# Attention and a mixture of experts on one core: 512-wide first-layer products, routing steps among the copies, another token layout, a shorter warm-up

## Chip, cores and metric

The kernel runs on one core of one Trainium2 chip. The metric is the device time of one execution in microseconds (us), as the median of several runs. Engines are named as in the profile: PE (TensorE; PEld is its weight load), DVE (VectorE), ACT (ScalarE), POOL (GpSimd), SP (SyncE).

## What is computed

Causal attention in blocks of 64 (8 batches, 8 heads, 576 rows, 64 columns a head) gives 4608 rows of 512. Each row goes to the one expert of eight with the largest logit, through two layers of weights, and is scaled with that expert's probability.

```python
scores = scale * np.matmul(q, k.transpose(0, 1, 3, 2))
mask = block_i >= block_j
scores = np.where(mask, scores, -1000000000.0)
scores = scores - np.max(scores, axis=-1, keepdims=True)
attn = np.exp(scores)
attn = attn / (np.sum(attn, axis=-1, keepdims=True) + 1e-09)
return np.matmul(attn, v).astype(np.float32)
...
x = np.ascontiguousarray(attn_out.transpose(0, 2, 1, 3)).reshape(B * S, H * D)
...
logits = x @ w_gate + modality_bias[modality_id]
e_idx = np.argmax(logits, axis=1)
logits_s = logits - logits.max(-1, keepdims=True)
probs = np.exp(logits_s)
probs /= probs.sum(-1, keepdims=True) + 1e-09
gate_w = probs[np.arange(N), e_idx]
for e in range(E):
    mask = e_idx == e
...
    h = np.maximum(x[mask] @ w1[e], 0.0)
    out[mask] = gate_w[mask, None] * (h @ w2[e])
```

## The kernel before

**Slots.** The 64 heads are worked in 32 pairs, one pair in a slot (0 to 31), with a last slot 32. `run_slot` goes through the table `ORDER`, a hand-written order of names; each name has a stage, and a name of stage 1 works on the pair of the slot before. Every engine runs its own instructions in the order in which they are written. S0 to S3 (`scores`, L202, PE) fill banks 0 to 5; M0 to M4 (`maxima`, L209, DVE) take row maxima; E0 to E4 (`exps`, L222, ACT) take exponentials with row sums. V (`values`, L248, PE) multiplies the pair before with its values into banks o0 and b0. T0 to T5 (`transposes`, L229, PE) turn the exponentials, C0 to C5 (`copies`, L234; C0, C1, C5 on DVE, the others on ACT) bring them to SBUF. O (`turn_out`, L256 and L257, ACT), D (`inverse`, L274 and L275, DVE), B (`back`, L268, PE: turns the rows back and multiplies with the gate's weights) and Z0, Z1 (`rows`, L287 and L288, DVE) end the pair before. Z stands at the end of the table, so DVE does it at the start of the next slot, ahead of that slot's M0. Q (`scale`, L184) scales the next pair's queries on POOL; pair 0's are scaled on DVE in one operation (L181).

**Routing.** Four pairs make a batch of 576 rows. After the fourth, `routing` gives 19 small steps: logits (L314), their total by PE (L317, into b0), four bias additions (L321 to L324), the maximum, the expert's index, a weight from the exponentials (L336 on ACT, L357 to L373), stores, counts by PE (L353, L354), running sums (L363 to L387). Steps are taken from the list in order, at the names q1 to q6; PE's products wait for the name qp, their readers for qv. Up to three steps are taken at one name when the list is long, when it holds selection steps (`choose`, 22 of them after the third batch), or from slot 29 on. After the last step five scatters are due for each batch: DVE adds (`pi`, L394), and POOL issues an indirect DMA (L395) that writes row numbers into the experts' lists. One scatter is issued at V and one at T3 of each slot while any is due.

**Experts.** From slot 20 on weights are fetched and split into high and low parts (L584, L585 on POOL). The last slot mixes the end of the last pair with the first expert part. A part is 256 rows of one expert; 18 full parts and one of 128 rows follow each other. First layer (`up_products`, L706): for m2 = 0 to 3 one bank holds two halves a; each half sums over kc = 0 to 3 the products w high x x high, w high x x low, w low x x high, 256 columns wide. `up_relu` (L712 ACT, L713 DVE) makes the high and low part of the hidden rows. Then the next part's rows are turned (`turn_rows`, L688 to L692), and the second layer (`down`, L752) takes 2 x 24 products 512 wide. Three banks rotate for the first layer (`s_bank`), two for turned rows (`t_bank`).

**Start.** Twelve warm-up products (L532) run on PE ahead of the first scores.

Of the kernel before, what the change touches and what calls it, by code (L numbers as in the profile page):

```python
# [25 lines left out]
PPB = H // 2  # L26
# [43 lines left out]
ORDER = (  # L70
# [3 lines left out]
)  # L74
# [7 lines left out]
LAST = (  # L82
    ("+turn0", 0), ("V", 1), ("O", 1), ("D", 1), ("+up0", 0), ("+relu", 0), ("+fetch", 0), ("B", 1), ("Z0", 1), ("Z1", 1), ("+steps1", 0), ("+up1", 0), ("+relu", 0),
    ("+place", 0), ("+steps13", 0), ("+up2", 0), ("+relu", 0), ("+place", 0), ("+steps5", 0), ("+up3", 0), ("+place", 0), ("+relu", 0), ("+turn1", 0), ("+fetch", 0), ("+fetch", 0),
)
# [22 lines left out]
def attention_moe(ctx, tc, qk, vr, bkw, mid, mb, w1, w2, cf, ci, ld, out):  # L108
# [160 lines left out]

    def inverse(p):  # L270
        d = pairs[p]
        den = sml.tile([128, NSUB], F32, name="den")
        d.inv = sml.tile([128, NSUB], F32, name="inv")
        dve.scalar_tensor_tensor(den, d.sums, GUARD, d.long, ALU.add, ALU.add)  # L274
        dve.reciprocal(d.inv, den)  # L275

# [22 lines left out]
    def routing(b):  # L299
        xr, gl = xrs[b]  # L300
        g = Pair()
        tot = b0[:, TABLE : TABLE + NSUB * NE].rearrange("p (s e) -> p s e", s=NSUB)
        ps = b0[:, TABLE : TABLE + 80]

        def t(shape, dt=F32, **k):
            return sml.tile(shape, dt, bufs=2, **k)
# [4 lines left out]

        def logits():
            g.l0 = t([128, NSUB, NE], name="l0")
            dve.tensor_reduce(g.l0, gl, AX.X, ALU.add)  # L314

        def total():
            pe.matmul(tot, ii, g.l0, start=True, stop=True)  # L317

        def biased():
            by = bias[:, 5 * b : 5 * b + 5, :]  # L320
# [17 lines left out]
        def hits():  # L338
            dve.tensor_tensor(eq, lg, bc(g.mx), ALU.is_equal)

        def hit_index():
            dve.tensor_tensor(eq, eq, iom40, ALU.mult)

# [31 lines left out]
        def stores():  # L375
            queue = nc.sync
            queue.dma_start(xrows[S * b : S * b + 512, 512:XW].rearrange("(c p) w -> p c w", p=128), g.wt[:, 0:4])
            queue.dma_start(xrows[S * b + 512 : S * b + S, 512:XW], g.wt[64:128, 4])
            g.idt = t([128, 5, IW], I32, name="idt")
            queue.dma_start(g.idt, ci[b].rearrange("p (c w) -> p c w", c=5))  # L380

# [64 lines left out]
    def emit(name, p):  # L446
        one = {
            "L": lambda: load(p), "Q": lambda: scale(p), "V": lambda: values(p), "O": lambda: turn_out(p), "D": lambda: inverse(p), "B": lambda: back(p),
            "Z0": lambda: rows(p, 0), "Z1": lambda: rows(p, 1),
        }  # L450
# [40 lines left out]
    def run_slot(slot):  # L491
# [3 lines left out]
        for name, stage in LAST if slot == NPAIR else ORDER:  # L495
            p = slot - stage
            if placing and slot < NPAIR and name in ("V", "T3"):
                g, c = placing.pop(0)
                g(c)
            for what in EARLY_STEPS.get((slot, name), ()):  # L500
                if ex is None:
                    ex = Experts(ctx, tc, cst, scratch, btmp, con["edges"], xrows, idlist, idf, w1, w2, out, sel, run, base8, pick, dot, banks, (o0, banks[5]), placing, staging, extra, xrb, lambda kind: any(getattr(f, "kind", "") == kind for f in steps))
                ex.early(what)
# [8 lines left out]
            if name[0] == "q":  # L512
                kind = "" if name[1].isdigit() else name
                kinds = (kind,) if kind else ("", "c")
                quick = bool(steps) and getattr(steps[0], "kind", "") == "c"
                for _ in range(1 if kind else 3 if quick else 3 if slot >= HURRIED else 1 + (len(steps) > 20)):
                    if slot > 1 and steps and getattr(steps[0], "kind", "") in kinds:
                        steps.pop(0)()
                continue
# [3 lines left out]
            if name == "Z1" and p % PPB == PPB - 1:  # L523
                steps = steps + routing(p // PPB)
                if p // PPB == EARLY - 1:
                    choose(Later(dve, steps))

    engines = {ET.PE, ET.Activation, ET.DVE, ET.Pool}
# [16 lines left out]
class Experts:  # L545
    def __init__(self, ctx, tc, cst, scratch, btmp, edges, xrows, idlist, idf, w1, w2, out, sel, run, base8, pick, dot, banks, ys, placing, staging, extra, xrb, steps_left):
# [13 lines left out]
        self.w["a", 1] = [[cut(1024 * (4 * x + c), 2) for c in range(4)] for x in range(2)]  # L560
        self.xth, self.xtl = cut(1024 * 8, 4), cut(1024 * 9, 4)
        self.hidden = [[cut(1024 * (10 + i) + 512 * x, 2, 512) for x in range(2)] for i in range(4)]
# [3 lines left out]
    def s_bank(self):  # L566
        self.sbank += 1
        return self.banks[(self.sbank - 1) % 3]

    def t_bank(self):  # L570
        self.tbank += 1
        return self.banks[3 + (self.tbank - 1) % 2]

# [124 lines left out]
    def up_products(self, s, m2):  # L698
        nc = self.nc
        wh, wl = self.w[s.name, 0]  # L700
        hp = self.s_bank().rearrange("p (a t) -> p a t", a=2)
        for a in range(2):
            ms = slice(256 * m2 + 128 * a, 256 * m2 + 128 * a + 128)
            mm = [(w, kc, x) for kc in range(4) for w, x in ((wh, self.xth), (wh, self.xtl), (wl, self.xth))]
            for i, (w, kc, x) in enumerate(mm):
                nc.tensor.matmul(hp[:, a, :], w[:, kc, ms], x[:, kc, :], start=i == 0, stop=i == len(mm) - 1)  # L706
        s.hp.append(hp)

    def up_relu(self, s):
        hh, hl = self.next_hidden()  # L710
        hp = s.hp.pop(0)
# [141 lines left out]


def _constants():
    p, j = np.indices((128, 128))
    late = np.arange(128) < 64
    ranks = np.broadcast_to(np.arange(NE) - NE, (128, 5, NE))
    seen = ranks.copy()
    seen[late, 4] = 100  # L860
    inv = np.zeros((128, 5))
    inv[late, 4] = BIG
    first = np.ones((128, NE, 5))
# [12 lines left out]
    cf = np.concatenate([con[n].reshape(128, -1) for n, _ in PARTS], axis=1).astype(np.float32)  # L876
    at = np.array([0, 128, 256, 384, 448])
    ci = (np.arange(B)[:, None] * S + at)[:, None] + np.arange(128)[None, :, None]
    ci = np.repeat(ci[..., None], IW, axis=3)
# [3 lines left out]
def _prepare(q, k, v, moe_modality_id, moe_w_gate, moe_modality_bias, moe_w1, moe_w2):  # L883
# [11 lines left out]
    ids = moe_modality_id.reshape(B, S)  # L895
    mid = np.zeros((128, B, 5), ids.dtype)
    mid[:, :, 0:4] = ids[:, 0:512].reshape(B, 4, 128).transpose(2, 0, 1)
    mid[:, :, 4] = np.tile(ids[:, 512:576].transpose(1, 0), (2, 1))
    mb = np.broadcast_to(moe_modality_bias.reshape(1, 2 * NE), (128, 2 * NE))
# [13 lines left out]
```

## Time and profile before

| | us |
|---|---|
| median of 3 runs | 742.62 (742.12 to 743.21) |
| profiled execution | 741.8, span 740.1 |
| PE / PEld busy | 723.7 / 630.2 |
| DVE / ACT / POOL busy | 345.7 / 332.4 / 243.5 |

The span begins with the first record of the profile and ends with the last; 1.7 us of the profiled execution lie outside it. The granted clock of PE is 0.996 of full speed on average over the span. Bars in the profile's timeline are merged where one line's instructions follow each other (x96 is 96 of them); the idle time before an instruction stands in brackets with what ended it.

### The profile page before, as it was taken

To read this page: it belongs to the slowest core of one execution; us is meant where nothing else is said; L and a number is where in the kernel's file an instruction comes from. 1 tells how busy PE (TensorE), PEld (TensorE's weight loads), DVE (VectorE), ACT (ScalarE), POOL (GpSimd) and SP (SyncE) were. 2 spreads that over 40 slices of the span, in tenths; PEclk is the share of its full clock that TensorE was granted. 3 is DMA by queue.
4 is the path that set the end of the run, shared out by engine and by line. 5 is a ranking of instruction groups with operands and counts; after the bars stand their busy time and mean duration, and the time that the engine had idled before them with its cause. 6 is when DMAs were issued, how large, how long until landed. Compare 5 with 4: busy or idle time off the path is not lost. (4 is left out here: it accounts for less than half of the span.)

```text
span 740.1 us, 19430 instructions
## 1 busy us (share of the span) xinstructions
PE 723.7 (98%) x7800; PEld 630.2 (85%) x7800; DVE 345.7 (47%) x1038; ACT 332.4 (45%) x974; POOL 243.5 (33%) x326
## 2 busy tenths in 40 slices
PE   8999999999999998999999999999999999999995
PEld 4888888777888887998899988999889988899794
DVE  5888888898899987513122011220222112221220
ACT  5888877777878877221222212321222212222220
POOL 2223342434398964245223222232111221112101
PEclk9999999999999999999999999999999999999998
DMA  5477455545776673313222022222122121201000
GB/s 187 129 208 220 119 170 136 175 106 158 183 226 190 229 211 72 86 59 79 82 72 85 31 86 72 72 72 72 57 72 72 59 86 58 72 29 48 29 15 20
DMA packets 41916, 77.80 MB, mean 105 GB/s; under 512 B 12170, under 2 KB 24266, under 8 KB 41824
## 3 DMA queue, kind: packets, MB, share of 16 engines
q1 hardware_dynamic: 34336, 57.02, 26.7%
q0 software_dynamic: 7488, 19.52, 8.4%
q8 instruction: 62, 1.02, 0.6%
q14 instruction: 30, 0.25, 0.1%
HBM read 54.86 MB, written 22.25 MB: 104 GB/s over the span
## 5 line engine op out<-in xcount | busy, mean ns | idle before, releaser
L713 DVE SCALAR_TENSOR_TENSOR extra<-bank,extra 128x512 fp32r<-128x512 f32 x72 | 49.8, 692 | 317.3 <-ACT extra L712 315.9
L222 ACT ACTIVATE pm<-bank,nm 128x512 f32<-128x512 f32 (+3 forms) x320 | 155.7, 502 | 64.6 <-DVE nm L209 59.0
L209 DVE TENSOR_REDUCE nm<-bank 128x1 f32<-128x512 f32 (+3 forms) x320 | 120.5, 448 | 4.0 <-PE bank L202 4.0
L706 PE MATMUL bank<-extra 128*128 128x256 f32 x960 | 116.0, 281 | 0.0
L706 PEld LDWEIGHTS bank<-extra 128*128 128x128 f32 x960 | 115.1, 188 | 1.0 <-issue 0.2
L712 ACT ACTIVATE extra<-bank 128x512 fp32r<-128x512 f32 x72 | 43.1, 598 | 151.4 <-PE bank L706 148.2
L229 PE MATMUL bank<-cf,pm 128*128 128x128 f32 (+1 forms) x736 | 91.2, 277 | 2.3 <-ACT pm L222 2.2
L184 POOL TENSOR_SCALAR q<-raw 128x144 f32<-128x144 f32 x124 | 68.0, 576 | 70.6 <-DMA raw<-qk 57.5
L706 PE MATMUL bank<-extra,w0hb 128*128 128x256 f32 x512 | 91.1, 280 | 0.0
L202 PE MATMUL bank<-raw,q 64*64 64x512 f32 (+7 forms) x1280 | 90.1, 407 | 0.8 <-POOL wt L373 0.6
L229 PEld LDWEIGHTS bank<-cf,pm 128*128 128x128 f32 (+1 forms) x736 | 78.1, 139 | 12.3 <-ACT pm L222 6.4
L202 PEld LDWEIGHTS bank<-raw,q 64*64 64x64 f32 x1280 | 56.9, 134 | 29.1 <-issue 20.7
L706 PEld LDWEIGHTS bank<-extra,w0hb 128*128 128x128 f32 x512 | 79.0, 188 | 0.7
L248 PE MATMUL b<-pt,v 64*64 64x64 f32 (+3 forms) x896 | 75.6, 266 | 1.0 <-DVE lg L324 0.9
L248 PE MATMUL o<-pt,v 64*64 64x64 f32 (+3 forms) x896 | 71.4, 262 | 1.2 <-DVE gl L288 1.2
L706 PE MATMUL bank<-extra,w0lb 128*128 128x256 f32 x256 | 71.8, 280 | 0.0
L755 POOL DMA_INDIRECT out<-scratch,ids_b x17 | 16.9, 995 | 161.8 <-ACT scratch L754 161.8
L234 DVE COPY pt<-bank 128x512 f32<-128x512 f32 (+1 forms) x96 | 58.9, 640 | 15.5 <-PE bank L229 9.7
L222 ACT ACTIVATION_READ_ACCUMULATOR pm<-bank,nm 128x1 f32 x320 | 65.3, 204 | 0.0
L395 POOL DMA_INDIRECT idlist<-idt,pi x40 | 40.5, 1012 | 65.8 <-DVE pi L394 47.5
L752 PE MATMUL o<-extra 128*128 128x512 f32 x240 | 57.3, 394 | 0.0
L248 PEld LDWEIGHTS b<-pt,v 128*64 128x64 f32 (+1 forms) x896 | 53.9, 136 | 3.6 <-DVE lg L324 1.1
(148 smaller groups left out, 997.0 us busy)
## 6 DMA issues: line engine op xcount, KB each, us to landing
raw<-qk SPq DMA_DIRECT2D x31, 576.0 KB
v<-vr SPq DMA_DIRECT2D x32, 384.0 KB
staging<-w SPq DMA_DIRECT2D x24, 256.0 KB
staging<-w SPq DMA_DIRECT2D x12, 512.0 KB
xrows<-xr SPq DMA_DIRECT2D x16, 256.0 KB
xrows<-xr SPq DMA_DIRECT2D x32, 128.0 KB
idlist<-btmp SPq DMA_DIRECT2D x8, 304.0 KB
xrows<-xr SPq DMA_DIRECT2D x16, 64.0 KB
```

The source lines that it names most:

```text
L184: pool.tensor_scalar(d.q[:, i : i + 144], d.raw[:, i : i + 144], SCALE, None, ALU.mult)
L202: pe.matmul(place(s, a, b)[64 * t : 64 * t + 64], d.q[hs, D * s : D * s + D], d.k[hs, a:b], start=True, stop=True)
L209: dve.tensor_reduce(d.nm[:, i : i + 1], place(s, a, b), AX.X, ALU.max, negate=True)
L222: act.activation(d.pm[:, o : o + b - a], place(s, a, b), AF.Exp, bias=d.nm[:, s : s + 1], scale=1.0, accum_out=total)
L229: pe.transpose(banks[g][0:m, 128 * i : 128 * i + 128], d.pm[:, o : o + m], idf)
L234: dve.tensor_copy(dst, src) if g in ON_DVE else act.copy(dst, src)
L248: pe.matmul(o.rearrange("p (n c) -> p n c", c=64), d.v[rows, h, block, :], x, start=start, stop=stop)
L395: last = pool.indirect_dma_start(idlist[:], bass.IndirectOffsetOnAxis(ap=g.pi[c], axis=0), g.idt[:, c, :], None, bounds_check=NROW - 1, oo ...
L706: nc.tensor.matmul(hp[:, a, :], w[:, kc, ms], x[:, kc, :], start=i == 0, stop=i == len(mm) - 1)
L712: self.nc.scalar.activation(hh, hp, AF.Relu)
L713: self.nc.vector.scalar_tensor_tensor(hl, hp, 0.0, hh, ALU.max, ALU.subtract)
L752: nc.tensor.matmul(y, s.hs[m][x][:, ts], self.part(w, 1, m // 2)[:, m % 2, :], start=n == 0, stop=n == len(mm) - 1)
```

## The change

Five things.

1. **First layer.** x high and x low lie side by side (`xt`), so one product of width 512 with the high weights serves both; the low weights' product with x high stays 256 wide and adds to the bank's low half. One half a fills one bank: 64 instead of 96 products per part. `up_relu` first adds the two halves of a bank on DVE (`hs`), twice, then takes ACT's relu and DVE's difference, twice each, 256 wide. `s_bank` rotates over four banks, `t_bank` over bank 4 and b0.
2. **Layout of the routing.** Each partition holds other tokens (`_tokens`), so that the total is two products of 64 x 40 into bank 5 and the bias is one addition. Hit and index are one step: 18 steps. The index load moves to the first step, four stores instead of two.
3. **Order of the steps.** q1 to q6 stand among the copies, after C1 and around C5, qv after C5; D is split. One step is taken at each name. The chain to the scatters comes first, 13 steps; weights and stores come behind it (and behind `choose`, for the third batch). Scatters are issued at T3 and B instead of V and T3. The last slot takes 1, 7, 5, 5 steps instead of 1, 13, 5.
4. **Warm-up** of 8 products instead of 12.
5. **First queries** scaled in two operations, columns 384 to 575 first.

```diff
-HURRIED = 29
+PLACED = 13
-NWARM = 12
+NWARM = 8
-TABLE = 400
+TABLE = 384
 ORDER = (
-    ("S0", 0), ("S1", 0), ("Q", -1), ("M0", 0), ("qv", 1), ("E0", 0), ...
-    ("L", -2), ("V", 1), ("q1", 1), ("E4", 0), ("O", 1), ("q2", 1), ("q3", 1), ("q4", 1),
...
+    ("T0", 0), ("C0", 0), ("T1", 0), ("C1", 0), ("q1", 1), ("D0", 1), ("q2", 1), ("D1", 1), ("T2", 0), ("C2", 0), ("q3", 1), ("q4", 1), ("T3", 0), ("C3", 0), ("T4", 0), ("C4", 0), ("T5", 0), ("qp", 1), ("C5", 0),
+    ("qv", 1), ("B", 1), ("q5", 1), ("q6", 1), ("Z0", 1), ("Z1", 1),
...
-            dve.tensor_scalar(d.q, d.raw[:, 0:S], SCALE, None, ALU.mult)
+            for i, j in ((384, S), (0, 384)):
+                dve.tensor_scalar(d.q[:, i:j], d.raw[:, i:j], SCALE, None, ALU.mult)
...
-            pe.matmul(tot, ii, g.l0, start=True, stop=True)
+            for t in range(2):
+                pe.matmul(tot[64 * t : 64 * t + 64], ii[:, 64 * t : 64 * t + 64], g.l0[:, 4 * t : 4 * t + 5], start=True, stop=True)
...
-            dve.tensor_tensor(lg[0:64, 0:4], tot[0:64, 0:4], by[0:64, 0:4], ALU.add)
-            dve.tensor_tensor(lg[64:128, 0:2], tot[64:128, 5:7], by[64:128, 0:2], ALU.add)
-            dve.tensor_tensor(lg[64:128, 2:4], tot[64:128, 4:8:3], by[64:128, 2:4], ALU.add)
-            dve.tensor_tensor(lg[:, 4], tot[:, 8], by[:, 4], ALU.add)
+            dve.tensor_tensor(lg, tot, bias[:, 5 * b : 5 * b + 5, :], ALU.add)
...
-            if placing and slot < NPAIR and name in ("V", "T3"):
+            if placing and slot < NPAIR and name in ("B", "T3"):
...
+        self.xt = extra[:, 1024 * 8 : 1024 * 10].rearrange("p (a x t) -> p a x t", a=4, x=2)
+        self.xth, self.xtl = self.xt[:, :, 0], self.xt[:, :, 1]
...
-        return self.banks[(self.sbank - 1) % 3]
+        return self.banks[(self.sbank - 1) % 4]
...
-            mm = [(w, kc, x) for kc in range(4) for w, x in ((wh, self.xth), (wh, self.xtl), (wl, self.xth))]
-            for i, (w, kc, x) in enumerate(mm):
-                nc.tensor.matmul(hp[:, a, :], w[:, kc, ms], x[:, kc, :], start=i == 0, stop=i == len(mm) - 1)
+            low = hp[a][:, 0:SLOT]
+            for kc in range(4):
+                if kc == 3:
+                    nc.tensor.matmul(low, wl[:, kc, ms], self.xth[:, kc], start=False, stop=False)
+                nc.tensor.matmul(hp[a], wh[:, kc, ms], self.xt[:, kc].rearrange("p x t -> p (x t)"), start=kc == 0, stop=kc == 3)
+                if kc < 3:
+                    nc.tensor.matmul(low, wl[:, kc, ms], self.xth[:, kc], start=False, stop=False)
...
-        self.nc.scalar.activation(hh, hp, AF.Relu)
-        self.nc.vector.scalar_tensor_tensor(hl, hp, 0.0, hh, ALU.max, ALU.subtract)
+        sums = [self.cst.tile([128, SLOT], F32, name="hs", bufs=3) for _ in range(2)]
+        for hs, hp in zip(sums, s.hp.pop(0)):
+            self.nc.vector.tensor_reduce(hs, hp.rearrange("p (x t) -> p t x", x=2), AX.X, ALU.add)
+        for a, hs in enumerate(sums):
+            self.nc.scalar.activation(hh[:, a], hs, AF.Relu)
+            self.nc.vector.scalar_tensor_tensor(hl[:, a], hs, 0.0, hh[:, a], ALU.max, ALU.subtract)
```

DVE before, from the copies of the slot that issues the first batch's first scatter to the rows of the pair (pp is the last routing step, pi a scatter's index, xr and gl the rows of Z):

```order
L390 TENSOR_REDUCE pp<-eq 128x5
L234 COPY pt_110<-bank_92 128x512
L234 COPY pt_110<-bank_93 128x512
L274 SCALAR_TENSOR_TENSOR den<-sums,long_67 128x9
L275 RECIPROCAL inv<-den 128x9
L394 TENSOR_TENSOR pi_1307<-pp,cf 128x1
L234 COPY pt_110<-bank_97 128x384
L287 TENSOR_TENSOR xr_82<-o_98,inv 128x5x64
```

DVE after, at the same place, which is one slot earlier:

```order
L236 COPY pt_111<-bank_93 128x512
L391 TENSOR_REDUCE pp<-eq 128x5
L276 SCALAR_TENSOR_TENSOR den<-sums,long_66 128x9
L279 RECIPROCAL inv<-den 128x9
L357 TENSOR_REDUCE sm<-ex 128x5
L360 TENSOR_SCALAR sm<-sm 128x5
L395 TENSOR_TENSOR pi_1168<-pp,cf 128x1
L236 COPY pt_111<-bank_97 128x384
L395 TENSOR_TENSOR pi_1169<-pp,cf 128x1
L372 RECIPROCAL sm<-sm 128x5
L291 TENSOR_TENSOR xr_82<-o_98,inv 128x5x64
```

Two weight steps now stand ahead of the first scatter's index, and a second scatter's index follows the last copy.

POOL before, the five scatters of the second batch among the scalings of the queries (each row of q is one pair's):

```order
L395 DMA idlist<-idt,pi_2550 38912x16
L184 TENSOR_SCALAR q_102<-raw_100 128x144 x4
L395 DMA idlist<-idt,pi_2551 38912x16
L395 DMA idlist<-idt,pi_2552 38912x16
L184 TENSOR_SCALAR q_103<-raw_101 128x144 x4
L395 DMA idlist<-idt,pi_2553 38912x16
L395 DMA idlist<-idt,pi_2554 38912x16
```

POOL after, the same five:

```order
L396 DMA idlist<-idt,pi_2409 38912x16
L396 DMA idlist<-idt,pi_2410 38912x16
L186 TENSOR_SCALAR q_103<-raw_101 128x144 x4
L396 DMA idlist<-idt,pi_2411 38912x16
L396 DMA idlist<-idt,pi_2412 38912x16
L186 TENSOR_SCALAR q_102<-raw_100 128x144 x4
L396 DMA idlist<-idt,pi_2413 38912x16
```

In both programs two scatters stand together on POOL; before they are those of V and T3 of one slot, after they are those of T3 and B.

PE after, the first half a and the beginning of the second of one m2 (before it is one row, `L706 MATMUL bank_94<-extra 128x256 x24`, for both halves):

```order
L710 MATMUL bank_94<-extra 128x512
L712 MATMUL bank_94<-extra 128x256
L710 MATMUL bank_94<-extra 128x512
L712 MATMUL bank_94<-extra 128x256
L710 MATMUL bank_94<-extra 128x512
L712 MATMUL bank_94<-extra 128x256
L709 MATMUL bank_94<-extra 128x256
L710 MATMUL bank_94<-extra 128x512
L710 MATMUL bank_95<-extra 128x512
```

The 24 products of 256 columns are 8 of 512 and 8 of 256, and the two halves lie in two banks.

## Rows read from the trace of the kernel before

**Rows 1.** Windows: length, then PE, PEld, DVE, ACT, POOL busy (instructions), PEclk, DMA.
```profile
14.42:282.99 268.57, 266.42 (x4679) 220.51 (x4679) 236.40 (x791) 213.65 (x759) 132.23 (x221) 1.00 0.60 172
...
323.32:683.95 360.63, 360.63 (x2382) 330.54 (x2380) 73.85 (x135) 87.90 (x140) 89.27 (x77) 1.00 0.22 66
```

**Rows 2.** Timeline of the start; columns: start us, length us, engine, line, operation, idle before.
```profile
0.86 0.40 SPq L170 DMA_DIRECT2D raw<-qk  x1
...
1.33 0.41 SPq L171 DMA_DIRECT2D raw<-qk  x1
...
1.46 5.28 PE L532 MATMUL b<-scratch,ones 128*128 128x512 bf16 x12 [1.46 <-DVE long L160]
...
3.99 0.46 DVE L181 TENSOR_SCALAR q<-raw 128x576 f32<-128x576 f32 x1 [2.55 <-DMA raw<-qk]
...
6.67 2.93 PE L202 MATMUL bank<-raw,q 64*64 64x512 f32 x40
```

**Rows 3.** Timeline at two slot starts: 110.90, an ordinary one, and 119.45 with a scatter.
```profile
110.90 0.60 PE L202 MATMUL bank<-raw,q 64*64 64x512 f32 x2
...
111.28 0.49 DVE L287 TENSOR_TENSOR xr<-o,inv 128x320 f32<-128x320 f32 x1 [0.33 <-PE o L268]
...
118.91 1.05 POOL L395 DMA_INDIRECT idlist<-idt,pi  x1 [8.04 <-DVE pi L394]
...
119.45 0.59 PE L202 MATMUL bank<-raw,q 64*64 64x512 f32 x2
...
120.46 0.49 DVE L287 TENSOR_TENSOR xr<-o,inv 128x320 f32<-128x320 f32 x1 [0.84 <-PE o L268]
...
128.69 0.59 PE L202 MATMUL bank<-raw,q 64*64 64x512 f32 x2
```

**Rows 4.** Waits of the program: us in total, times, longest.
```profile
DVE xr L287 <- PE o L268: 5.5, 12, 1.0
...
DVE xr L287 <- PE bank L202: 3.9, 4, 1.2
```

**Rows 5.** Windows of single slots, from one slot's first score product to the next slot's.
```profile
57.35:66.29 8.94, 8.94 (x172) 7.22 (x162) 7.52 (x28) 6.75 (x26) 2.18 (x4) 1.00 1.00 327
156.19:166.03 9.84, 9.40 (x172) 7.48 (x167) 9.52 (x45) 7.34 (x27) 4.25 (x6) 1.00 0.57 128
...
272.56:282.99 10.43, 9.88 (x173) 8.23 (x165) 8.19 (x33) 7.58 (x27) 4.81 (x8) 1.00 0.79 216
```

**Rows 6.** Timeline of one expert part, from 485.43 to the next part's first product.
```profile
485.43 11.52 PE L706 MATMUL bank<-extra 128*128 128x256 f32 x96
...
496.79 1.03 PE L688 MATMUL bank<-cf,xr 128*128 128x128 f32 x8
...
497.58 5.73 PE L752 MATMUL o<-extra 128*128 128x512 f32 x24
...
503.15 0.61 PE L752 MATMUL bank<-extra 128*128 128x512 f32 x2
...
508.59 0.40 PE L706 MATMUL bank<-extra,w0hb 128*128 128x256 f32 x2
```

**Rows 7.** Groups by line and form: operations of like shape as the new evacuation.
```profile
L713 DVE SCALAR_TENSOR_TENSOR extra<-bank,extra 128x512 fp32r<-128x512 f32 x72 | 49.8, 692 | 317.3 <-ACT extra L712 315.9 <-issue 1.3
...
L209 DVE TENSOR_REDUCE nm<-bank 128x1 f32<-128x512 f32 x64 | 43.6, 681 | 4.0 <-PE bank L202 4.0
...
L287 DVE TENSOR_TENSOR xr<-b,inv 128x256 f32<-128x256 f32 x32 | 13.3, 415 | 0.0
```

**Rows 8.** Groups by line and form: one of the four bias additions.
```profile
L324 DVE TENSOR_TENSOR lg<-b,bias 128x8 f32<-128x8 f32 x8 | 1.3, 167 | 0.1
```

**Rows 9.** Timeline of the last slot, two scatters one after the other.
```profile
291.58 1.00 POOL L395 DMA_INDIRECT idlist<-idt,pi  x1 [0.30 <-DVE pt L234]
...
292.88 0.98 POOL L395 DMA_INDIRECT idlist<-idt,pi  x1 [0.30 <-issue]
...
294.70 0.49 DVE L287 TENSOR_TENSOR xr<-o,inv 128x320 f32<-128x320 f32 x1 [2.21 <-PE bank L688]
```

More of the change, by code (lines that the diff above doesn't have):

```diff
@@ L268, in back, with inverse @@
                         pe.matmul(bank[t : t + 64, VW * i : VW * i + VW], ot[hs, 64 * c : 64 * c + 64], bk[hs, q, :], start=True, stop=True)
-    def inverse(p):
+    def inverse(p, part):
         d = pairs[p]
[L272 to L275, printed above, removed]
+        if part == 0:
+            d.den = sml.tile([128, NSUB], F32, name="den")
+            dve.scalar_tensor_tensor(d.den, d.sums, GUARD, d.long, ALU.add, ALU.add)
+        else:
+            d.inv = sml.tile([128, NSUB], F32, name="inv")
+            dve.reciprocal(d.inv, d.den)
     def rows(p, k):
@@ L301, in routing @@
         g = Pair()
-        tot = b0[:, TABLE : TABLE + NSUB * NE].rearrange("p (s e) -> p s e", s=NSUB)
-        ps = b0[:, TABLE : TABLE + 80]
+        ps = banks[5][:, TABLE : TABLE + 80]
+        tot = ps[:, 0:40].rearrange("p (c e) -> p c e", c=5)
         def t(shape, dt=F32, **k):
@@ L376, in stores @@
             queue = nc.sync
[L377 to L380, printed above, removed]
+            place = xrows[S * b : S * b + S, 512:XW].rearrange("(s p) w -> p s w", p=64)
+            queue.dma_start(place[:, 0:7:2], g.wt[0:64, 0:4])
+            queue.dma_start(place[:, 5], g.wt[0:64, 4])
+            queue.dma_start(place[:, 1:4:2], g.wt[64:128, 1:3])
+            queue.dma_start(place[:, 7:9], g.wt[64:128, 3:5])
         def place_run():
@@ L400, in place_sum @@
             placing.extend((scatter, c) for c in range(5))
-        return [logits, total, biased, top, shifted, hits, expo, hit_index, first, onehot, weight, weight_guard, weight_out, stores, counts, running, place_run, place_pick, place_sum]
+        return [logits, total, biased, top, shifted, hits, first, onehot, counts, running, place_run, place_pick, place_sum, expo, weight, weight_guard, weight_out, stores]
     sel = {}
@@ L447, in emit @@
         one = {
-            "L": lambda: load(p), "Q": lambda: scale(p), "V": lambda: values(p), "O": lambda: turn_out(p), "D": lambda: inverse(p), "B": lambda: back(p),
+            "L": lambda: load(p), "Q": lambda: scale(p), "V": lambda: values(p), "O": lambda: turn_out(p), "D0": lambda: inverse(p, 0), "D1": lambda: inverse(p, 1), "B": lambda: back(p),
             "Z0": lambda: rows(p, 0), "Z1": lambda: rows(p, 1),
@@ L501, in run_slot @@
                 if ex is None:
-                    ex = Experts(ctx, tc, cst, scratch, btmp, con["edges"], xrows, idlist, idf, w1, w2, out, sel, run, base8, pick, dot, banks, (o0, banks[5]), placing, staging, extra, xrb, lambda kind: any(getattr(f, "kind", "") == kind for f in steps))
+                    ex = Experts(ctx, tc, cst, scratch, btmp, con["edges"], xrows, idlist, idf, w1, w2, out, sel, run, base8, pick, dot, banks + [b0], (o0, banks[5]), placing, staging, extra, xrb, lambda kind: any(getattr(f, "kind", "") == kind for f in steps))
                 ex.early(what)
@@ L514, in run_slot @@
                 kinds = (kind,) if kind else ("", "c")
[L515 to L518, printed above, removed]
+                if slot > 1 and steps and getattr(steps[0], "kind", "") in kinds:
+                    steps.pop(0)()
                 continue
@@ L523, in run_slot @@
             if name == "Z1" and p % PPB == PPB - 1:
-                steps = steps + routing(p // PPB)
+                more = routing(p // PPB)
+                steps += more[0:PLACED]
                 if p // PPB == EARLY - 1:
                     choose(Later(dve, steps))
+                steps += more[PLACED:]
     engines = {ET.PE, ET.Activation, ET.DVE, ET.Pool}
@@ L567, in s_bank @@
         self.sbank += 1
-        return self.banks[(self.sbank - 1) % 3]
+        return self.banks[(self.sbank - 1) % 4]
     def t_bank(self):
         self.tbank += 1
-        return self.banks[3 + (self.tbank - 1) % 2]
+        return self.banks[4 + 2 * (self.tbank % 2)]
     def early(self, what):
@@ L852, in rest, with _tokens @@
                 self.down(s, i)
+def _tokens():
+    at = D * np.array([ROWS[0:5], ROWS[4:9]])
+    return (at[:, None] + np.arange(D)[None, :, None]).reshape(128, 5)
 def _constants():
     p, j = np.indices((128, 128))
-    late = np.arange(128) < 64
+    late = np.arange(128) >= 64
     ranks = np.broadcast_to(np.arange(NE) - NE, (128, 5, NE))
     seen = ranks.copy()
-    seen[late, 4] = 100
+    seen[late, 0] = 100
     inv = np.zeros((128, 5))
-    inv[late, 4] = BIG
+    inv[late, 0] = BIG
     first = np.ones((128, NE, 5))
@@ L876, in _constants @@
     cf = np.concatenate([con[n].reshape(128, -1) for n, _ in PARTS], axis=1).astype(np.float32)
[L877 to L878 removed]
+    ci = np.arange(B)[:, None, None] * S + _tokens()
     ci = np.repeat(ci[..., None], IW, axis=3)
```

19 lines of the change are left out of this document (7 added, 12 removed), and 4 rows, old and new, of the table ORDER.

## Prediction

> **What bounds the kernel now.** I read the windows of the whole program first, then the timeline at the places that the change touches, then the groups by form for prices. TensorE (PE) carries the time: it is busy for 266.4 of the 268.6 us between slots 1 and 31, and for all of the 360.6 us that most of the expert parts take [rows 1]. So a change counts where it takes work off PE, or where it changes what PE waits for. Three stages differ.
>
> *Start.* Twelve warm-up products run from 1.46 us and the first score product starts at 6.67, though the queries had landed by 3.99 [rows 2]. The warm-ups, not the data, are last there.
>
> *Slots.* An ordinary slot takes 8.55 us (110.90 to 119.45 [rows 3]), and that is PE's own work. The 30 slots from 14.42 to 282.99 take 268.57 us [rows 1], 12.1 us more than 30 x 8.55. Where do they go? In the slot that starts at 119.45, VectorE (DVE) begins L287 1.01 us after the slot's start instead of 0.38, having waited for PE's last product of L268, and the slot takes 9.24 us [rows 3]. A scatter (L395 on GpSimd, POOL) had started at 118.91, across the boundary: PE's release came 1.55 us after that start. I call it a **hold**. In the waits L287 stands behind L268 for 5.5 us in 12 places and behind L202 for 3.9 in 4 [rows 4]; an ordinary one is 0.33, so about eight are long. Other slots are long from routing steps: 8.94 us in slot 6, where four bias additions stand between the maxima M0 and M1, 9.84 in slot 17, where three selection steps are popped at each place, 10.43 in slot 30, where three routing steps at a place meet [rows 5].
>
> *Experts.* A part takes 23.16 us: 96 products of L706 in 11.36 (485.43 to 496.79), 8 transposes, 48 products of L752 from 497.58 to 508.59 [rows 6]. That is 118.3 ns for a 256-wide product and 229.4 ns for a 512-wide one. ACT and DVE are far from busy there (88 and 74 of 361 us [rows 1]).
>
> **First-layer products.** For each output half and each kc, three 256-wide products (354.9 ns) become one 512-wide and one 256-wide: 229.4 + 118.3 = 347.7 ns. The saved 7.2 ns occur 4 x 2 x 4 = 32 times in a part and 18 parts are full: 576 x 7.2 ns = **4.2 us**. The columns are the same, only a third of the instructions goes, so little can be saved. Bounds: the first 24 products of L752 take 5.57 us (497.58 to 503.15 [rows 6]), 232 ns each, and at 232 the saving is 2.6 us. If a 256-wide product is its 106.7 ns of columns at the 2.4 GHz level plus 11.6 ns per instruction, a 512-wide one takes 225 ns and 6.7 us are saved. I take 229.4, which is measured with a weight load before each product, as here.
>
> The Trainium skill, page "TensorE: Matmul & The Clock Gate", section "Wait — 56ns, not 53.3ns?", gives N/2.4 GHz + about 2.5 ns from start to start on a warm array. By it the three products take 327.5 and the two 325.0 ns, an estimate from that page of 1.4 us saved in all; the trace has 118.3 where the rule has 109.2, and 229.4 where it has 215.8, so by the measurement the fixed part is larger than the rule's.
>
> The price of the edit lies on DVE. Per m2 it did one 692 ns operation (L713) behind one of ACT; now it does two reductions of a whole bank and two 256-wide operations. The nearest rows are 681 ns for a reduction over 512 columns of PSUM and 415 for a 256-wide operation [rows 7]: 2 x 0.68 + 2 x 0.42 = 2.2 us, while PE needs 8 x 347.7 ns = 2.78 us per m2. The strided reduction itself has no row. Were it twice as slow, the sum would be 3.6 us; the last hidden rows are asked for only by the 19th product of L752, 18 x 0.229 = 4.1 us after the first, so up to about 3.7 us per m2 stays hidden, and I cost it at nothing. Four rotating banks instead of three, two per m2, leave one m2 of lead: the two reductions free them within 1.4 us of the 2.78.
>
> **Start.** Four warm-ups fewer, 0.44 us each by the 5.28 us of twelve [rows 2], let PE start at about 4.95. The first score products need q's columns from 384 on: a third of the 0.46 us scaling, ready at about 4.2. The keys are issued 0.47 us after the queries (0.86 and 1.33), so I estimate that they land between 4.5 and 5.0. The chain of maxima and exponentials then starts 1.2 to 1.7 us earlier. The score products up to about 7.2 us run at the low level of the clock, 1.2 GHz (the warm-ups' 0.44 us for 512 columns), which costs part back; if the rise comes later, more. I take **1.2 us**, bounds 0 and 2.0.
>
> **Slots.** (a) The bias additions go from four to one and out of the M chain: seven slots at 8.94 - 8.55 = 0.39, less what remains, about 0.3 each: 2.1 us. The steps now lie after C1 and C5, where DVE waits for PE's transposes; an addition costs 167 ns [rows 8], and DVE was busy for 7.52 of slot 6's 8.94 us. (b) Slots 17 and 30 lie 1.29 and 1.88 us over the ordinary; single steps give back about 1.2 in slot 30 and 0.8 each in 17 and its like neighbour 18: 2.8 us. (c) The scatters move from V to B, those at T3 stay. Now each T3 scatter that stands behind two routing steps starts up to 0.4 us later, and the B scatter follows it at once on POOL. Eight strong holds become some eleven, each about 0.5 us, five of them 0.3 later: -3.0 us. The B scatter starts about 0.7 us into the next slot and can hold the first score products back from M0, which stands at about 1.3: 7 x 0.2 = -1.4 us. The logits' table is in bank 5 and needs two small products instead of one, 0.1 us of PE at most, beside others. Sum of (a) to (c): 2.1 + 2.8 - 4.4 = **0.5 us** saved, bounds below. D in two halves, the earlier index load and a fourth store cost nothing: DVE waits there, and SP's queue has no waiter within microseconds. The last slot has seven instead of thirteen routing steps ahead of its third up product, worth 0.3 us by the 0.1 to 0.2 us of such a step; it gains reductions that PE covers.
>
> **Sum.** 4.2 + 1.2 + 0.5 + 0.3 = 6.2 us off the profiled execution of 741.8: 735.6. The median is 0.8 above that execution: **736.4 us**.
>
> **Rivals.**
> *Paired scatters (the other side).* In the last slot two scatters follow each other, 291.58 and 292.88, and L287 starts at 294.70, 1.82 us after the second and 3.1 after the first [rows 9]: the hold went on through both. The changed order makes such pairs at T3 and B of slots 7, 8, 11, 12, 15, 16 and 31 (in the slots between, POOL is late anyway with the experts' weights). First scatter at 8.0 us of the slot as at 118.91, the second 1.3 later, L287 1.82 after that: 2.6 us into the next slot instead of 0.38, less 0.3 of slack: 1.9 us, of which 0.5 is in the sum. Seven times 1.4 is 10 us: 746. It is slower than before from 1.1 us a pair on. For it: the one pair of the trace at a boundary. Against: a release that falls before the second scatter takes hold, 1.55 after the first and 0.25 after the second's start, ends it. At half the price it gives 741.
> *Holds vanish.* With DVE's order changed around the boundary the release may no longer be late: 4.4 us return, and the eight old holds with them: about 730.
> *Width brings nothing.* If the time above the columns grows with the width, so that a 512-wide product takes 2 x 118.3 ns, the experts' gain is 0: 740.6. The 229.4 ns of L752 speaks against it. The page's rule, above, would make it 739.2.
> *Evacuation binds.* If the reduction takes 1.5 us or more, or a hold delays it, DVE passes 3.7 us per m2 and PE waits in 18 parts: every 0.1 us above that costs 18 x 4 x 0.1 = 7 us. A factor of over two against the 681 ns row is needed.
>
> **How the numbers follow.** Forecast as summed 0.57; holds vanish 0.10; paired scatters 0.20 (of it 0.09 slower, 0.07 within the bound, 0.04 still faster); width brings nothing 0.10 (0.08 faster, 0.02 within); evacuation binds 0.03, of it 0.02 slower. About 0.2%, 1.5 us, is what a measurement of this kernel can tell from no change. Faster: 0.57 + 0.10 + 0.04 + 0.08 + 0.01 = 0.80; within: 0.09; slower: 0.11. The range of the forecast alone is 732 (6.7 for the products, 2.0 for the start) to 740.5. Down to 728 it takes in vanished holds with the better product price; up to 743.5 the pairs at up to two thirds of their price.
>
> **What the changed profile would show.** In the timeline of a part, two products from start to start 347 to 348 ns apart in sum, the part at 22.9 us instead of 23.16, and DVE's reduction at 0.6 to 0.8 us. First score product at about 5.0, slot 1 about 1.2 us before 14.42. L287 at slot starts after slots 7, 8, 11, 12: at 1.0 to 1.4 us by the forecast, at 2.6 by the pairs, at 0.4 if holds vanish. What would make it wrong: a longer idle row before L287 or M0, or PE idle in the up products.

## Result

The changed kernel takes 750.45 us (median of 6 runs, 748.59 to 752.59), the kernel before 743.29 in the same runs: a ratio of 1.0093 (95% interval 1.0074 to 1.0112). It is slower by 7 us, where 6 us faster was forecast. The profiled execution has a span of 749.0 us, against 740.1.

Where the 8.9 us of the span come from is read by stage. The stage marks are the first score product (S0) of slot 0, of slot 1 and of slot 31, the first product of the first expert part, and PE's last product.

| stage, us | before | after | difference |
|---|---|---|---|
| up to slot 1 | 14.42 | 13.51 | -0.9 |
| slots 1 to 30 | 268.57 | 280.86 | +12.3 |
| slot 31 and the last slot's beginning | 15.54 | 15.52 | 0 |
| experts, to PE's last product | 432.6 | 430.3 | -2.3 |

Windows of the changed kernel (length, then PE, PEld, DVE, ACT and POOL busy with their instruction counts, granted clock, DMA): the 30 slots, and 15 expert parts.

```profile
13.51:294.37 280.86, 275.35 (x4691) 221.35 (x4694) 234.02 (x764) 212.60 (x757) 131.83 (x221) 1.00 0.56 164
334.59:681.50 346.91, 346.91 (x1801) 294.97 (x1800) 163.02 (x311) 99.48 (x195) 85.44 (x73) 1.00 0.22 67
```

The first line answers to the slots of [rows 1]: 12.3 us longer, and PE is idle for 5.5 us, where it was idle for 2.2. The other 9 us stand in the profile as longer busy time of nearly the same number of products, so idle time alone does not show the loss. In the parts PE has no idle time, as before; 346.91 / 15 is 23.13 us a part. DVE went from a fifth to nearly half busy there and nobody waits for it.

*Start.* Timeline of the changed kernel:

```profile
1.46 3.57 PE L533 MATMUL b<-scratch,ones 128*128 128x512 bf16 x8 [1.46 <-DVE long L161]
...
4.25 0.53 DVE L183 TENSOR_SCALAR q<-raw 128x192 f32<-128x192 f32 x2 [2.81 <-DMA raw<-qk]
...
5.11 3.71 PE L204 MATMUL bank<-raw,q 64*64 64x512 f32 x40
```

Eight warm-ups end at 5.0, the first score product starts at 5.11 instead of 6.67 [rows 2], slot 1 at 13.51. Of 1.56 us at the first product 0.91 are left at slot 1: the 40 products shown take 3.71 us instead of 2.93 [rows 2]. In both profiles the record of the clock at its full level (2.4 GHz) begins at 7.18 us, and more of the score products now stand ahead of it. That time differs from one execution to the next: it is 5.43 us in the profiles of the third and fourth run below, which start slot 1 at 13.60 with the old start and at 12.69 with the new, again 0.91 apart.

*Experts.* Timeline of one part of the changed kernel, its first products, and the first of the next part; then the groups of the evacuation by form:

```profile
472.91 0.39 PE L710 MATMUL bank<-extra 128*128 128x512 f32 x1
473.14 0.28 PE L712 MATMUL bank<-extra 128*128 128x256 f32 x1
...
473.26 0.39 PE L710 MATMUL bank<-extra 128*128 128x512 f32 x1
473.49 0.28 PE L712 MATMUL bank<-extra 128*128 128x256 f32 x1
...
495.97 0.39 PE L710 MATMUL bank<-extra 128*128 128x512 f32 x1
```

```profile
L719 DVE TENSOR_REDUCE hs<-bank 128x256 f32<-128x512 f32 x144 | 98.2, 687 | 194.2 <-PE bank L710 194.1
...
L722 DVE SCALAR_TENSOR_TENSOR extra<-hs,extra 128x256 fp32r<-128x256 f32 x144 | 68.4, 479 | 12.8 <-ACT extra L721 12.0 <-issue 0.2
...
L721 ACT ACTIVATE extra<-hs 128x256 fp32r<-128x256 f32 x144 | 60.2, 418 | 146.5 <-DVE hs L719 146.5
```

A 512-wide product is 0.23 us from start to start, a 256-wide one 0.118. Over a part 64 products take 11.26 us, 11.36 before [rows 6], and the whole part 23.06 instead of 23.16. The strided reduction costs 687 ns, hardly more than the row over 512 columns [rows 7].

*Slots.* Timeline of the changed kernel around the start of slot 9 (POOL's scatters, PE's first score product, DVE's L291, which was L287 before), and windows of five slots, 9, 13, 16, 17 and 30:

```profile
83.34 1.04 POOL L396 DMA_INDIRECT idlist<-idt,pi  x1 [3.52 <-DVE pi L395]
...
83.89 0.59 PE L204 MATMUL bank<-raw,q 64*64 64x512 f32 x2
...
84.69 0.97 POOL L396 DMA_INDIRECT idlist<-idt,pi  x1 [0.30 <-issue]
...
86.29 0.49 DVE L291 TENSOR_TENSOR xr<-o,inv 128x320 f32<-128x320 f32 x1 [2.17 <-issue]
```

```profile
83.89:94.42 10.53, 10.07 (x174) 7.55 (x167) 7.41 (x24) 7.05 (x27) 4.40 (x7) 1.00 0.60 160
121.91:132.22 10.31, 10.20 (x173) 7.82 (x168) 7.48 (x24) 7.27 (x27) 4.09 (x7) 1.00 0.61 159
150.40:160.88 10.48, 10.02 (x169) 7.54 (x165) 7.70 (x29) 7.03 (x26) 4.41 (x7) 1.00 0.17 59
160.88:171.16 10.28, 9.98 (x169) 7.62 (x165) 7.78 (x30) 7.04 (x26) 4.09 (x7) 1.00 0.51 119
283.82:294.37 10.55, 10.55 (x171) 7.71 (x166) 8.00 (x31) 6.85 (x26) 4.60 (x8) 1.00 0.96 269
```

Two scatters follow one another, 83.34 and 84.69, and DVE's first operation of Z, which needs PE's products of the slot before, starts at 86.29: 2.41 us into the slot and 1.60 after the second scatter's start. It had been idle for 2.17 us. An ordinary slot has 0.38, the hold of one scatter gave 1.01 [rows 3]. This is the wait of [rows 9], now at slots 9, 13, 16, 17 (2.41, 2.19, 2.60, 2.40 us), 30 and 31 (2.56 and 2.90; ahead of slot 31 the first of the two is the fetch of expert rows, L669, at 294.26).

It is PE's release that is late, and not DVE that stands still. The view puts the wait down to "issue", but the semaphore updates in the trace tell: PE's semaphore is updated at 83.41 and next at 86.21, while ACT's and DVE's are updated four times from 83.51 to 84.13. In all six places PE's stands still for 2.6 to 3.3 us, until 1.5 to 1.9 us after the second start; in slots 3 to 5, which have no scatter, it never does so for more than 2.2.

### The profile page after: what moved, and what is told of

It is laid out like the page before. It is cut to its first block, busy times and chain, and to the rows that moved or that the text cites. A ratio compares the mean times of both kernels' runs of the same rounds, so it can differ in the third digit from the quotient of the medians.

```text
span 749.0 us, 18662 instructions
## 1 busy us (share of the span) xinstructions
PE 730.3 (98%) x7236; PEld 602.2 (80%) x7236; DVE 450.0 (60%) x1223; ACT 349.0 (47%) x1046; POOL 243.2 (32%) x326
## 5 line engine op out<-in xcount | busy, mean ns | idle before, releaser
L719 DVE TENSOR_REDUCE hs<-bank 128x256 f32<-128x512 f32 x144 | 98.2, 687 | 194.2 <-PE bank L710 194.1
L721 ACT ACTIVATE extra<-hs 128x256 fp32r<-128x256 f32 x144 | 60.2, 418 | 146.5 <-DVE hs L719 146.5
L710 PE MATMUL bank<-extra 128*128 128x512 f32 x320 | 109.3, 397 | 0.0
L204 PE MATMUL bank<-raw,q 64*64 64x64 f32 (+7 forms) x1280 | 96.5, 410 | 1.0 <-issue 0.7
L710 PE MATMUL bank<-extra,w0hb 128*128 128x512 f32 x256 | 86.1, 394 | 0.0
L250 PE MATMUL b<-pt,v 64*64 64x64 f32 (+3 forms) x896 | 78.3, 267 | 1.1 <-issue 0.9
L722 DVE SCALAR_TENSOR_TENSOR extra<-hs,extra 128x256 fp32r<-128x256 f32 x144 | 68.4, 479 | 12.8 <-ACT extra L721 12.0
L712 PE MATMUL bank<-extra 128*128 128x256 f32 x240 | 67.2, 280 | 0.0
L710 PEld LDWEIGHTS bank<-extra 128*128 128x128 f32 x320 | 55.5, 188 | 7.9 <-issue 0.2
L250 PEld LDWEIGHTS o<-pt,v 128*64 128x64 f32 (+1 forms) x896 | 51.5, 135 | 7.4 <-issue 2.6
```

Of the source, the lines that this page charges most:

```text
L204: pe.matmul(place(s, a, b)[64 * t : 64 * t + 64], d.q[hs, D * s : D * s + D], d.k[hs, a:b], start=True, stop=True)
L250: pe.matmul(o.rearrange("p (n c) -> p n c", c=64), d.v[rows, h, block, :], x, start=start, stop=stop)
L710: nc.tensor.matmul(hp[a], wh[:, kc, ms], self.xt[:, kc].rearrange("p x t -> p (x t)"), start=kc == 0, stop=kc == 3)
L712: nc.tensor.matmul(low, wl[:, kc, ms], self.xth[:, kc], start=False, stop=False)
L719: self.nc.vector.tensor_reduce(hs, hp.rearrange("p (x t) -> p t x", x=2), AX.X, ALU.add)
L721: self.nc.scalar.activation(hh[:, a], hs, AF.Relu)
```

## Experiments

The theory after the result: **pairs**. Two scatters that follow each other on POOL hold back PE's releases through both. The rival: the **steps behind C5** stand ahead of Z on DVE (up to five operations) and push everything back. Two more were open: what products and start are worth by themselves, and what a better place would give. Four kernels ran first.

**Scatters back at V and T3, all else as changed.**

```diff
-if placing and slot < NPAIR and name in ("B", "T3"):
+if placing and slot < NPAIR and name in ("V", "T3"):
```

> The changed kernel with its scatters issued at V and T3, as before the change; all else as changed. Pairs theory (two scatters one after the other at T3 and B hold PE's release through both): the five slots of 10.3 us and more (9, 13, 16, 17, 30) fall to 9.3 or less, 1 to 1.5 us each, and the slots 22 to 29, whose first scatter waits behind the weight split, lose one of two scatters there; together 7 to 10 us, 741 to 743. Rival, the routing steps behind C5 (they stand ahead of L291 on VectorE): the time stays within 2 us of the changed kernel, 748 to 750.

745.24 us, ratio to the kernel before 1.0045 (1.0028 to 1.0062): 5.2 us less than the changed kernel by the medians, 3.6 by the two ratios. Windows of the 30 slots, of slot 31 with the last slot's beginning, and of slots 9 and 13; then the timeline ahead of slot 9, which starts at 82.47:

```profile
12.64:285.03 272.39, 268.45 (x4694) 219.66 (x4693) 235.54 (x773) 212.57 (x758) 131.28 (x219) 1.00 0.57 170
285.03:303.08 18.05, 16.20 (x220) 12.47 (x220) 9.39 (x32) 8.72 (x29) 6.39 (x7) 0.81 0.14 37
82.47:91.65 9.18, 9.17 (x173) 7.33 (x168) 7.46 (x24) 6.91 (x26) 4.39 (x7) 1.00 0.59 143
118.52:127.64 9.12, 9.12 (x173) 7.38 (x167) 7.40 (x24) 6.91 (x26) 4.40 (x7) 1.00 0.66 168
```

```profile
81.92 0.97 POOL L396 DMA_INDIRECT idlist<-idt,pi  x1 [1.44 <-DVE pi L395]
...
83.53 0.49 DVE L291 TENSOR_TENSOR xr<-o,inv 128x320 f32<-128x320 f32 x1 [0.89 <-PE bank L204]
```

The slots fall from 280.86 to 272.39, by 8.5 us, as the pairs theory has it: 9 and 13 from 10.53 and 10.31 to 9.18 and 9.12. The first scatter stands where it stood, 0.55 us ahead of slot 9; without the second L291 starts 1.06 us into the slot instead of 2.41. Not all arrives, and the 741 to 743 expected was missed, since slot 31 with what follows takes 18.05 instead of 15.52 (below, on the clock). The rival alone, 748 to 750, is out. But the slots still stand 3.8 us above those of before: slots 22 to 29 are 4.1 us longer than there and slot 30 1.5, the others 1.9 shorter. So 4.1 us there are not due to the scatters' new places (more on them below).

**The kernel before, scatters at B and T3.**

```diff
-if placing and slot < NPAIR and name in ("V", "T3"):
+if placing and slot < NPAIR and name in ("B", "T3"):
```

> The kernel before with one edit: scatters issued at B and T3 instead of V and T3. Pairs theory: the loss appears in the old order too, five to seven boundaries at about 1.4 us each, 750 to 753. Rival, the steps behind C5: nothing moves, 742 to 744.

755.59 us, 1.0184 (1.0167 to 1.0202): this one line costs 13 us in the old order too, more than the 750 to 753 expected. In its profile the 30 slots take 281.87 us, 13.3 more than before, and L287 starts 1.8 to 2.8 us into eight of them. The place of above in its timeline:

```profile
82.95 1.10 POOL L395 DMA_INDIRECT idlist<-idt,pi  x1 [8.04 <-DVE pi L394]
...
83.49 0.60 PE L202 MATMUL bank<-raw,q 64*64 64x512 f32 x2
...
84.35 0.97 POOL L395 DMA_INDIRECT idlist<-idt,pi  x1 [0.30 <-issue]
...
85.86 0.49 DVE L287 TENSOR_TENSOR xr<-o,inv 128x320 f32<-128x320 f32 x1 [2.13 <-issue]
```

L287 starts 2.37 us into the slot and 1.51 after the second scatter's start. No routing step was moved here, so the pair is enough.

**The new products alone.** `up_products`, `up_relu`, `xt` and the two bank rotations in the kernel before (the diff's lines).

> The kernel before with the new first-layer products and their evacuation alone. By the profile of the changed kernel, where a 512-wide product takes 232.6 ns, 576 times 4.7 ns are saved: 2.3 to 2.7 us, 740.8. If the evacuation were what the experts pay with, PE would show idle time in the up products and the time would stay at 743.

740.07 us, 0.9965 (0.9952 to 0.9978): 2.6 us gained. The experts take 430.1 us in its profile, as in the changed kernel.

**The new start alone.** `NWARM = 8` and the scaling in two parts in the kernel before.

> The kernel before with 8 warm-up products and the first queries scaled in two parts, nothing else. If the start is worth what the first slot shows, 0.9 us: slot 1 starts at 13.5 and the time is 742.4. If what the start gains is given back at the low clock or later, the time is 743.3.

741.23 us, 0.9986 (0.9974 to 0.9997): 1.0 us with an interval of 0.2 to 1.9.

Then the places themselves.

**The changed kernel, scatters at M2 and V.**

```diff
-if placing and slot < NPAIR and name in ("B", "T3"):
+if placing and slot < NPAIR and name in ("M2", "V"):
```

> The changed kernel with its scatters issued at M2 and V, so that none runs across a slot boundary and none follows another at once. If the hold only costs where it covers PE's last product of L268, L291 starts at 0.4 to 0.9 us in every slot and the slots fall by 9 us or more against the changed kernel: 740 to 742. What stays above an ordinary slot is then the price of the routing steps behind C5, 0.2 to 0.6 us in a slot with running sums. Rival: a hold costs wherever it falls, as the score products' releases are then late for the maxima: 744 to 748.

741.38 us, 0.9977 (0.9959 to 0.9995): 8 to 9 us below the changed kernel. In slots 9 to 18 the time above an ordinary slot falls from 10.7 us to 1.9; L291 starts at 0.4 to 1.1. The time above 8.55 that is left there, 0.2 to 0.4 us in the slots behind running sums, is the steps behind C5. But slot 30 takes 14.9 us, 4.3 more than in the changed kernel. SyncE's queue, POOL and PE in its timeline:

```profile
266.17 0.65 SPq L378 DMA_DIRECT2D xrows<-wt  x1
...
270.07 7.08 SPq L298 DMA_DIRECT2D xrows<-xr  x8
...
277.89 0.48 SPq L174 DMA_DIRECT2D raw<-qk  x1
...
284.46 2.18 POOL L186 TENSOR_SCALAR q<-raw 128x144 f32<-128x144 f32 x4 [8.20 <-DMA raw<-qk]
286.69 1.97 PE L204 MATMUL bank<-raw,q 64*64 64x512 f32 x8 [5.71 <-POOL q L186]
```

The four weight stores of the sixth batch (L378 and on) wait until 266.17 for the weights, which POOL copies behind a weight split; the eight stores of rows (L298) and the load of pair 31's queries stand behind them. The load is issued at 277.89, the scaling starts at 284.46, and PE stands still for 5.71 us. In the changed order weights and stores come behind the chain of steps to the scatters, so they meet the loads there.

**The kernel before with products, start and scatters at M2 and V.**

> The kernel before with the new first-layer products, the shorter warm-up and the two-part first queries, its old order of steps, and the scatters at M2 and V. The two parts measured alone give 2.5 and 1.3 us: 738.8. If the eight single holds at slot boundaries go as well, 0.5 us each: 734.5 to 735.5. If a hold costs as much among the maxima, 738 to 740.

734.72 us, 0.9893 (0.987 to 0.9915). The two parts alone would give 738.8, so the scatters' new places are worth about 4 us by the runs, as expected for eight single holds. The profiled execution, at 736.2 the slowest of the four, shows less: its 30 slots take 267.41 us, 1.2 below those of before. Slots 9 and 13 fall from 9.24 to 8.73, but slots 23 and 26 rise to 9.99 and 9.59. That the 4 us are the single holds is therefore not shown.

**The changed kernel, steps at their old names, scatters at M2 and V.** `ORDER` as before with D0 and D1 together, three selection steps at a name, and the last slot takes all the steps that are left at its last place.

> The changed kernel with the steps at their old names (q1 to q4 ahead of C0, qv after M0, D split but together, up to three selection steps at one name) and the scatters at M2 and V. It keeps the new token layout with one bias addition, 18 steps with the placing chain first, the new products and the new start. If the old places are the better ones and the layout is worth about 0.25 us in each slot with bias additions: 733 to 735, below the kernel that has the old layout. Rival: the steps among the copies were the gain and the old places cost 2 to 4 us: 737 to 740.

746.62 us, 1.0062 (1.0038 to 1.0086): worse than either expectation. L290, which is L287 of before, starts at 0.38 us in nearly every slot, so DVE is not late; yet slots 5, 9, 13 take 9.59 and 6, 10, 14 take 9.92 us. Waits of PE in it (us in total, times, longest):

```profile
PEld bank L323 <- DVE pt L235: 7.1, 7, 1.1
PE bank L323 <- DVE pt L235: 5.2, 7, 0.8
PE bank L352 <- DVE pt L235: 4.3, 6, 0.7
```

PE's totals and counts (L323, L352) wait for DVE's copy of the turned exponentials: C5 reads bank 5, and the table now lies in bank 5, in other columns. In the old order these products stand behind C5.

**The same with the table in b0.**

```diff
-TABLE = 384
+TABLE = 400
-        ps = banks[5][:, TABLE : TABLE + 80]
+        ps = b0[:, TABLE : TABLE + 80]
```

> The kernel of e8 with one more edit: the table of the totals and counts back in bank b0 (column 400) instead of bank 5. In e8 the slots 5, 6, 7, 9, 10, 11 and so on, those with a total or counts, took 0.6 to 1.4 us more than an ordinary one although VectorE was early. If PE waited there for C5 to leave bank 5, these slots fall by 0.5 to 1 us each, 21 of them, together 10 to 13 us: 733 to 736, and below the kernel with the old layout if its bias addition is worth what it seemed. Rival, the steps at their old names cost it by themselves: within 2 us of e8, 745 to 748.

731.53 us, 0.9856 (0.9826 to 0.9887): 15 us gained by two lines, and the fastest of all: 10.4 us below the kernel before in the same runs. Its 30 slots and its slot 9:

```profile
13.36:276.13 262.77, 262.40 (x4693) 217.91 (x4692) 233.09 (x764) 214.98 (x758) 131.91 (x220) 1.00 0.60 176
82.14:90.94 8.80, 8.80 (x173) 7.34 (x167) 7.64 (x24) 7.23 (x26) 2.99 (x4) 1.00 0.60 138
```

PE is idle for 0.4 of 262.8 us.

**The changed kernel at M2 and V, sixth batch's stores on POOL.** `queue = pool if b == 5 else nc.sync`.

> The kernel of e5 with the four weight stores of the sixth batch issued by GpSimd instead of SyncE. In e5 slot 30 took 14.9 us: PE waited 5.7 us for the queries of pair 31, scaled late because their load left SyncE's queue 5 us late, behind those stores, which waited for the weights. If that is the cause, slot 30 falls to 9 or 10 us and the time by 4 to 5.5 us: 736 to 737.5. Rival, the load is slow by the traffic of the other loads: slot 30 stays above 13 us, 741.

737.86 us, 0.9936 (0.9911 to 0.9961): 3.5 us less than without it, by the medians; the two intervals just overlap. The load of pair 31's queries is issued at 271.23 instead of 277.89:

```profile
271.23 0.42 SPq L174 DMA_DIRECT2D raw<-qk  x1
```

PE no longer waits for these queries, but slot 30 falls from 14.88 to 11.78 us and not to 9 or 10. The stores now stand ahead of two scatters on POOL, which come at 271.85 and 273.26, across the start of slot 30, and L291 starts 2.53 us into it: a pair again.

**The changed kernel with the table in b0.** The two lines above in the changed kernel.

> The changed kernel with the table of totals and counts in bank b0 (column 400) instead of bank 5, all else as changed. C5 no longer shares a bank with PE's small products, so that the slots with a total or counts get shorter by 0.1 to 0.3 us each, 2 to 4 us in all: 746 to 748. Rival, the bank does no harm where the products stand ahead of C5: 749 to 751.

758.35 us, 1.0239 (1.019 to 1.0287): 8 us worse than the changed kernel by the medians, where 2 to 4 less were expected; its 30 slots take 289.43 us, 8.6 more. Waits in it:

```profile
PEld b L270 <- DVE pos L365: 4.1, 7, 0.7
...
PE b L270 <- DVE pos L365: 3.1, 7, 0.6
...
PEld b L270 <- DVE lg L327: 2.4, 5, 0.7
```

With qp ahead of C5 the table in b0 stands ahead of B, which writes into b0 and so waits until DVE has read the table (pos, lg). In this program each bank suits one order only: bank 5 has qp ahead of C5, b0 has it behind.

## Why the prediction was wrong

**What failed: the price of scatters, (c) under slots.** The sum had -4.4 us for them and the likeliest case took the pair's hold as ending with the first scatter. It does not: at all six boundaries that two indirect DMAs in a row ran across, the hold went on through both. Moving the scatters back shortens the slots by 8.5 us (first run), and the one line that makes the pairs costs 13 us by itself in the old order (second run). The rival of paired scatters had the mechanism and the price at a boundary right, 2.6 us into the next slot against 2.2 to 2.9 measured; its total, 746, was still too low. It was given 0.20. The argument against it, that a release falling 0.25 us after the second scatter's start ends the hold, rested on no row, while the only pair of the trace at a boundary [rows 9] spoke for it.

**Counted too few.** The rival left out slots 22 to 29, "POOL is late anyway". There the time above an ordinary slot went from 1.3 to 9.2 us, which is 8.0 of the 12.3 us by which the slots grew. With the scatters back at V and T3 it is 5.4 (first run), so about half of the 8.0 is due to the scatters' new places. POOL is late there, so the two scatters run later in the slot and hold other releases. That is read from a trace, and no run isolates it: in the kernel with stores on POOL the scatters from M2 and V have come together behind a weight split, and C0 waits for a transposition that PE began at 210.9:

```profile
210.19 1.05 POOL L396 DMA_INDIRECT idlist<-idt,pi  x1 [0.16 <-issue]
...
211.55 0.98 POOL L396 DMA_INDIRECT idlist<-idt,pi  x1 [0.30 <-issue]
...
213.22 1.29 DVE L236 COPY pt<-bank 128x512 f32<-128x512 f32 x2 [2.32 <-PE bank L231]
```

1.67 us after the second scatter's start C0 begins, after 2.32 us idle. A place that keeps two scatters apart when POOL is on time does not do so when it is behind.

Of the seven boundaries named three did not come. Those of slots 7 and 11: the first scatter's index waited for the weight's steps, and the scatter started 0.3 us into the next slot, which then took 9.1 and 9.4 us. That of slot 31: the two scatters start at 305.49 and 306.81, and L291 runs at 305.76 without a wait. The pairs at the starts of slots 30 and 31 were not named.

**(a) and (b), the steps, were mis-sized too.** "Where DVE waits for PE's transposes" was right of C1, not of C5, behind which Z has no slack beyond 0.3 us. With the scatters at M2 and V slots 7, 11 and 15, where five operations stand between C5 and Z, start L291 at 0.9 to 1.1 us and take 8.8 to 8.9. Beside POOL's weight split it is worse. In slot 22 of the changed kernel no scatter is near, yet L291 starts 1.51 us into the slot, since one of the five operations took 0.75 us (last rows of this document); slot 25 is alike, 1.55 us there and 1.77 with the scatters back at V and T3. These are some of the 4.1 us that the first run leaves in slots 22 to 29; that they are all of them is not shown. The single bias addition gave what was forecast where its step keeps its old name: slot 6 takes 8.61 us in the fastest kernel instead of 8.94. The single pops gave less than (b) read into slots 17 and 18 (9.84 and 9.95 before): with three selection steps at a name these take 9.00 and 8.62 in the fastest kernel, with one at a name 8.55 each in the fifth run. So most of their excess was not the pops. Together (a) and (b) had 4.9 us; with the scatters at their old places (first run) slots 1 to 21 are 1.8 us shorter than before, and what slots 22 to 29 lose is more than that.

**SP's queue, costed at nothing, was wrong.** In the changed kernel it hardly shows (slot 30 is held by a pair anyway), but PE waits 2.11 us behind it in the first run and 5.71 in the fifth.

**Products: the term was mis-sized.** 2.6 us by the run, 2.3 by the profile, 4.2 forecast. The 512-wide product takes some 233 ns from start to start in the changed kernel's trace, not the 229.4 that one part gave for L752; over all parts L752 takes 231.7 in the kernel before. 2.6 was the lower bound of the text, at 232. By the rule of the Trainium skill, page "TensorE: Matmul & The Clock Gate", section "Wait — 56ns, not 53.3ns?" (N/2.4 GHz + about 2.5 ns), the gain would have been 1.4, an estimate, below the interval of 1.6 to 3.6 us.

**Evacuation at nothing, start 1.2: right.** Two reductions and two differences are 2 x 687 + 2 x 479 = 2.3 us of DVE per m2 against 2.8 of PE. The start gave 1.0 us by the run and 0.9 in the profiles, within its bounds.

**What stays open.** Why an indirect DMA on POOL holds PE's releases is not known. The rows show when: L287 or L291 starts 1.5 to 1.9 us after the start of the last scatter that holds it, single or second of a pair. Which of its parts (its descriptors, its transfer, the release's way) does it was not tried.

## What to carry to other kernels

Before moving an indirect DMA on POOL, list what stands next to it on POOL and which of PE's releases falls within 3 us of its start; keep two of them apart (2.0 to 2.7 us and clear of the boundary was enough in slots 8, 9, 12, 13, 16 and 17 of the fifth run), also for the case that POOL is late. A table in PSUM shares its bank's readers: in these programs a product into free columns waits for the copy of the others. A step moved in DVE's order takes its DMA stores along in SP's queue, ahead of loads that another slot needs.

## What the runs showed of the hardware that was not expected

*A short wait of PE can cost the clock.* In the first run the wait for pair 31's queries left PE idle for 2.11 us ahead of slot 31, and behind it the granted clock was at the half level (1.2 GHz) from 285.23 to 288.64. The same came again after a wait of 1.76 us (timeline, PE; then windows: length, PE busy, granted clock, DMA):

```profile
285.03 4.39 PE L204 MATMUL bank<-raw,q 64*64 64x512 f32 x39 [2.11 <-POOL q L186]
...
298.32 0.33 PE L250 MATMUL o<-pt,v 64*64 64x64 f32 x4 [1.76 <-DVE gl L292]
```

```profile
279.00:283.00 4.00, 3.91 (x65) 1.00 1.04 376
...
285.23:288.64 3.41, 3.41 (x26) 0.50 0.15 29
...
290.00:293.00 3.00, 3.00 (x43) 1.00 0.01 3
...
298.88:302.30 3.42, 3.42 (x40) 0.50 0.06 6
```

Slot 31 and the last slot's beginning ran at 0.81 on average (its windows above) and took 2.5 us longer than in the changed kernel, the wait of 1.76 us included. A wait does not always cost it: in the kernel before the same stretch, 282.99 to 298.53, ran at 1.00 with a wait of 1.19 us at 295.38. In the run of the products alone a wait of the same length, at 294.62, was followed by the half level from 295.56 to 298.97. What decides is not shown.

*A small operation of DVE can take longer beside one of POOL.* In the changed kernel one routing operation of 40 elements behind slot 21's C5, 0.22 us elsewhere, took as long as POOL's subtraction that began at the same time:

```profile
206.56 0.73 POOL L587 TENSOR_TENSOR extra<-staging,extra 128x256 fp32r<-128x256 f32 x1
...
206.59 0.75 DVE L384 TENSOR_TENSOR eq<-cum,pos 128x40 f32<-128x40 f32 x1
...
207.69 0.48 DVE L291 TENSOR_TENSOR xr<-o,inv 128x320 f32<-128x320 f32 x1
```
